# Attention feeding an MLP: weight loads placed between the first pairs' casts, transposes moved inside a pair, and the first MLP tile begun earlier

## The chip, the cores and the metric

The kernel runs on one core of a Trainium2 chip. The metric is the device time of one execution, in microseconds. Eight runs of the kernel before took 435.03 to 438.9 us, with a median of 437.28 us. The profile is of one execution that took 436.74 us; its recorded span is 435.0 us.

The core has five engines that work side by side, each through its own queue in order: PE (matrix products, with PEld for loading the stationary operand), DVE and ACT (elementwise work), POOL (elementwise work and DMA issues) and SP (DMA issues only). Sixteen DMA engines move the data.

## The reference

```python
scores = scale * np.matmul(q, k.transpose(0, 1, 3, 2))      # 8 batches, 12 heads, 448 x 448, head size 64
attn = np.exp(scores - max) / (sum + 1e-09)
attn_out = np.matmul(attn, v)                               # [8, 12, 448, 64]
x = attn_out.transpose(0, 2, 1, 3).reshape(3584, 768)
h = x @ w_in                                                # 768 x 2048
g = np.maximum(0.01 * h, h)
out = g @ w_out                                             # 2048 x 768
```

All inputs and the output are float32 in memory; the kernel multiplies in bf16. The kernel leaves out the subtraction of the maximum, whose factor cancels in the division, and gets the sum from a column of ones beside v.

## The kernel before, in words

**Units.** Two heads of one batch make a pair, so there are 48 pairs `u`, six to a batch. The MLP's 3584 rows are cut into eight tiles at multiples of 128: the first has 384 rows, the others 384 to 512. MLP tile i can begin when all six pairs of batch i have left their output, turned, in `xT`.

**A pair's way.** `load` brings q, k and v by three DMAs of 224 KB each on SP's queue (the very first k on ACT's). `cast` turns them to bf16 on POOL: q and k into `qkb` (L109, L110; 4 buffers), v into one of five v tiles (L111). q and k are then turned so that the head dimension lies on partitions: by PE in `transposes` (eight products into the single PSUM buffer `tr`, L159, then one DVE copy, L162) for the pairs below `NPE` = 10, by a DMA transpose on SP's queue for the rest. `scores` makes one 112-row chunk of scores for both heads (L171) in one of two PSUM buffers; `expo` takes its exponential on ACT (L180). There are four chunks, so four exponentials to a pair. `pv` multiplies them with v for one head (16 small products into the single buffer `pv`, L189), and DVE divides (L196, L197). `x_transposes` turns the pair's output into `xT`: by PE and `tr` again for pairs below 7 (L210, L211), by DMA from then on.

**Weights.** `w_in` and `w_out` are cast to bf16 by the DMA itself, issued from POOL's queue by `load_w` in eight pieces: four column quarters of `w_in`, then four row quarters of `w_out` (L123). One piece is issued ahead of the loop, one after each cast in slots 0, 1, 2, and the four `w_out` pieces in pairs 5 to 8.

**The order.** It is written out by hand. Each pair has eight slots, `s0` to `s7`, and slots of one `u` mix work of three pairs: scores of `u`, `pv` of `u-1`, x transposes of `u-2`, cast of `u+3`, load of `u+5`, and the PE transposes of `u+1` in the last slot. `steps` is the list of all slots. `begin[i]` is the step after which MLP tile i starts; from there its products (`mlp`, one product per `yield`) are dealt out evenly over the steps up to `begin[i+1]`. Tile 0 starts in pair 7 after its slot 1: `begin[0]` = 8 x 7 + 7 - 5 = 58. It is dealt out over 53 steps, first `h` for the 16 row blocks (L232, L237), then, for each 128 rows, two column halves of the output (L244, L249), and `store` on SP's queue.

**Buffers that set the order of transfers.** There are five load buffers of each of q, k and v, so SP can issue the load of pair u+5 when pair u is cast. The queue of SP is in order: a DMA transpose or a store in it stands ahead of the loads issued after it.

Of the kernel before, what the change touches and what calls it, by code (L numbers as in the profile page):

```python
# [9 lines left out]
F32 = mybir.dt.float32  # L10
BF16 = mybir.dt.bfloat16
# [5 lines left out]
def kernel(  # L17
# [9 lines left out]
    nc = tc.nc  # L27

    B, H, S, D = q.shape
    DM, DF = moe_w_in.shape  # L30
    P = 128
    HP = H // 2
# [3 lines left out]
    MD = DF // P  # L36
    NW = DM // 2
    NU = B * HP
    scale = 1.0 / float(D) ** 0.5

    cuts = [((b * S) // P) * P for b in range(B)] + [B * S]
# [3 lines left out]
    const_pool = ctx.enter_context(tc.tile_pool(name="const", bufs=1))  # L45
# [10 lines left out]
    o_pool = ctx.enter_context(tc.tile_pool(name="o", bufs=3))  # L56
# [4 lines left out]
    ps_mm = ctx.enter_context(tc.tile_pool(name="ps_mm", bufs=2, space=PSUM))  # L61
# [20 lines left out]
    w_out_sb = w_pool.tile([P, MD, DM], BF16)  # L82
    w_in_v = moe_w_in.rearrange("(ko ki) n -> ki ko n", ki=P)
    w_out_v = moe_w_out.rearrange("(ko ki) n -> ki ko n", ki=P)
# [6 lines left out]
    def load(u, queues=(nc.sync,) * 3):  # L91
        if u >= NU:
            return
        b, hp = divmod(u, HP)
        raw[u] = []
        for a, name, eng in zip((q, k, v), ("fq", "fk", "fv"), queues):
            t = ld_pool.tile([SC, 2, NSC, D], F32, name=name)
            eng.dma_start(  # L98
                out=t.rearrange("p h so d -> p h (so d)"),
                in_=a[b, 2 * hp:2 * hp + 2].rearrange("h (p so) d -> p h (so d)", so=NSC),  # L100
            )
            raw[u].append(t)

    def cast(u, by=(nc.gpsimd.tensor_copy,) * 3):
        if u >= NU:
            return
        fq, fk, fv = raw.pop(u)
        qk_sb[u] = cast_pool.tile([SC, 2, NSC, 2, D], BF16, name="qkb")
        by[0](qk_sb[u][:, 0].rearrange("p so h d -> p h so d"), fq)  # L109
        by[1](qk_sb[u][:, 1].rearrange("p so h d -> p h so d"), fk)  # L110
        by[2](v_sb[u % NV][:, :, :, :D], fv)  # L111

    w_steps = []
    for i in range(4):
        w_steps.append((w_in_sb[:, :, ts(i, DF // 4)], w_in_v[:, :, ts(i, DF // 4)]))
    for i in range(4):
        w_steps.append((w_out_sb[:, ts(i, MD // 4), :], w_out_v[:, ts(i, MD // 4), :]))

    def load_w(n=1):
        for _ in range(n):  # L120
            if w_steps:
                o, i = w_steps.pop(0)
                nc.gpsimd.dma_start(out=o, in_=i)  # L123

    load(0, (nc.sync, nc.scalar, nc.sync))
    for i in range(1, 5):
        load(i)
    ident = const_pool.tile([P, P], BF16)
    make_identity(nc, ident)
    for t in v_sb:  # L130
# [10 lines left out]

    x_t = {}

    NPE = 10

    def turn(dst, src):
        nc.sync.dma_start_transpose(out=dst.rearrange("p (c s) -> p c s", s=SC), in_=src)

    def dma_transposes(u):
        if NPE <= u < NU:  # L150
            turn(qkT[u % NQ][:, :QL], qk_sb[u].rearrange("p i so h d -> p (i so h d)"))

    def transposes(u):
        if u >= min(NPE, NU):
            return
        tr = ps_tr.tile([P, 2, S], BF16, name="tr")
        for i in range(2):
            for so in range(NSC):
                nc.tensor.transpose(  # L159
                    tr[:, i, ts(so, SC)], qk_sb[u][:, i, so], ident[:SC, :SC]  # L160
                )
        nc.vector.tensor_copy(qkT[u % NQ][:, :QL], tr.rearrange("p i s -> p (i s)"))  # L162
# [3 lines left out]
    def scores(u, c):  # L166
        ps = ps_s.tile([P, 2, 512], F32, name="sc")
        t = qkT[u % NQ]
        sc_t[u, c] = ps
        for j in range(2):  # L170
            nc.tensor.matmul(  # L171
                ps[:, j, :S],
                t[j * D:(j + 1) * D, S + c * SC:S + c * SC + P],
                t[j * D:(j + 1) * D, :S],
                start=True, stop=True,
            )

    def expo(u, c):
        e = e_sb[u % NE][:, :EL].rearrange("p (j c s) -> p j c s", j=2, c=NSC)
        nc.scalar.activation(e[:, :, c, :], sc_t.pop((u, c))[:SC, :, :S], AX.Exp, scale=scale)  # L180

    def pv(u, j):

        e, vt = e_sb[u % NE], v_sb[u % NV]
        ps = ps_pv.tile([P, NSC, D + 1], F32, name="pv")
        for qc in range(NSC):
            for c in range(NSC):
                at = (j * NSC + c) * S + qc * SC
                nc.tensor.matmul(  # L189
                    ps[:, qc, :], e[:, at:at + P], vt[:, j, c, :],  # L190
                    start=(c == 0), stop=(c == NSC - 1),
                )
        if j == 0:
            x_t[u] = x_pool.tile([SC, NSC, 2, D], BF16, name="x")
        rec = r_pool.tile([SC, NSC, 1], F32, name="rec")
        nc.vector.reciprocal(rec, ps[:SC, :, D:])  # L196
        nc.vector.tensor_mul(  # L197
            x_t[u][:, :, j, :], ps[:SC, :, :D], rec.to_broadcast([SC, NSC, D])
        )

    def x_transposes(u):
        b, hp = divmod(u, HP)
        at = b * S % NX
        dst = xT[:, hp, at:at + S]
        if u >= NPE - 3:
            turn(dst, x_t.pop(u).rearrange("p so h d -> p (so h d)"))
            return
        tr = ps_tr.tile([P, 2, S], BF16, name="tr")
        for so in range(NSC):
            nc.tensor.transpose(tr[:, 0, ts(so, SC)], x_t[u][:, so], ident[:SC, :SC])  # L210
        nc.vector.tensor_copy(dst, tr[:, 0, :])  # L211


    def store(o, t0):

        done = 0
        while done < P:
            b, j = divmod(t0 + done, S)
            so, p = divmod(j, SC)
            n = min(SC - p, P - done)  # L220
            dst = out[b * S:(b + 1) * S].rearrange("(p so) n -> so p n", so=NSC)
            nc.sync.dma_start(out=dst[so, p:p + n], in_=o[done:done + n, :])
            done += n

    def mlp(i):
        n = cuts[i + 1] - cuts[i]
        at = cuts[i] % NX
        h = h_pool.tile([P, MD, 4 * P], BF16, name="h")
        for m in range(MD):
            ps = ps_mm.tile([P, 4 * P], F32, name="mm")  # L230
            for kk in range(KD):
                nc.tensor.matmul(  # L232
                    ps[:, :n], w_in_sb[:, kk, ts(m, P)], xT[:, kk, at:at + n],
                    start=(kk == 0), stop=(kk == KD - 1),
                )
                if kk == KD - 1:
                    nc.scalar.activation(h[:, m, :n], ps[:, :n], AX.Prelu, alpha=0.01)  # L237
                yield n
        for c in range(n // P):
            o = o_pool.tile([P, DM], F32, name="o")  # L240
            for w in range(2):
                ps = ps_mm.tile([P, 4 * P], F32, name="mm")
                for m in range(MD):
                    nc.tensor.matmul(  # L244
                        ps[:, :NW], h[:, m, ts(c, P)], w_out_sb[:, m, ts(w, NW)],
                        start=(m == 0), stop=(m == MD - 1),
                    )
                    if m == MD - 1:
                        nc.vector.tensor_copy(o[:, ts(w, NW)], ps[:, :NW])  # L249
                    yield NW  # L250
            store(o, cuts[i] + c * P)


    def slots(u):

        on = u < NU

        def s0():
            if on:
                scores(u, 0)  # L260
                scores(u, 1)
                expo(u, 0)

        def s1():
            if on:
                expo(u, 1)
            if 2 <= u <= NU + 1:
                x_transposes(u - 2)
            dma_transposes(u + 2)

        def s2():
            if 1 <= u <= NU:
                pv(u - 1, 0)

        def s3():
            load(u + 5)

        def s4():
            if on:
                scores(u, 2)  # L280
                scores(u, 3)
                expo(u, 2)

        def s5():
            if on:
                expo(u, 3)
            cast(u + 3)
            if u <= 2 or 5 <= u <= 8:
                load_w()

        def s6():
            if 1 <= u <= NU:
                pv(u - 1, 1)

        def s7():
            if u + 1 < NU:
                transposes(u + 1)

        return [s0, s1, s2, s3, s4, s5, s6, s7]

    steps = [s for u in range(NU + 2) for s in slots(u)]

    begin = [8 * (HP * (i + 1) + 1) + 7 - 5 * (i == 0) for i in range(B)]
    assert begin[B - 1] == 8 * (NU + 1) + 7
    transposes(0)
    for s in steps[:begin[0]]:
        s()
    for i in range(B):
        work = steps[begin[i]:begin[i + 1]] if i + 1 < B else []
        n = cuts[i + 1] - cuts[i]  # L310
# [42 lines left out]
```

## Time and profile before

| | |
|---|---|
| median of 8 runs | 437.28 us |
| profiled execution | 436.74 us, span 435.0 us |
| PE busy | 410.2 us (94%), 3678 instructions |
| ACT busy | 230.0 us (53%) |
| DVE busy | 97.8 us (22%) |
| POOL busy | 91.3 us (21%) |
| read from memory, written to it | 45.61 MB, 11.01 MB |

A row by stage gives, after the stretch and its length, the busy time of each engine with its number of instructions, the granted clock of PE, the mean busy share of the DMA engines and the rate. A row of the time line gives the start, the length, the engine, the line of the program, the operation, its result and operand with sizes, the count, and in brackets the idle time of the engine before it and what ended it. Two successive products overlap in the record, so prices of PE work are best taken from start to start.

### The profile page before, as it was taken

How to read it: one execution, taken by the hardware profiler on the slowest of the kernel's cores; microseconds unless marked ns; L12 is line 12 of the kernel's file. 1: busy time of each engine (PE TensorE's matmuls, PEld its weight loads, DVE VectorE, ACT ScalarE, POOL GpSimd, SP SyncE). 2: the span in 40 equal slices, each digit the busy share in tenths (PEclk: the TensorE clock that was granted, in tenths of full speed). 3: DMA queues.
4: the chain of work that ended last, by engine and by line, in shares of the span. 5: the costliest groups of instructions: out<-in, count | busy, mean ns of one | idle time of the engine just before them, and what ended most of it. 6: DMA issues, size and time to landing. Idle time of an engine off the chain costs nothing.

```text
span 435.0 us, 8908 instructions
## 1 busy us (share of the span) xinstructions
PE 410.2 (94%) x3678; PEld 225.4 (52%) x3692; DVE 97.8 (22%) x266; ACT 230.0 (53%) x322; POOL 91.3 (21%) x168
## 2 busy tenths in 40 slices
PE   3767969999999999999999999999999999999995
PEld 1445535554455555554455555554445555554563
DVE  1343311321122211331123211331112311320021
ACT  4677645456743577447653377447654377304300
POOL 5535504231112113131112213122111200000000
PEclk9999997999999999999999999999999999999998
DMA  9999999876646775776656766786556440230022
GB/s 226 252 245 270 244 183 250 231 189 152 122 103 171 162 174 128 155 210 151 121 132 169 136 167 155 145 213 147 121 145 174 72 101 13 57 83 4 0 74 72
DMA packets 99273, 64.35 MB, mean 148 GB/s; under 512 B 58272, under 2 KB 95648, under 8 KB 99232
## 3 DMA queue, kind: packets, MB, share of 16 engines
q1 hardware_dynamic: 93744, 57.25, 55.8%
q0 software_dynamic: 5248, 6.29, 8.5%
q8 instruction: 29, 0.48, 0.5%
q10 hardware_dynamic: 240, 0.23, 0.2%
q14 instruction: 12, 0.10, 0.1%
HBM read 45.61 MB, written 11.01 MB: 130 GB/s over the span
## 4 chain that ended last, share of the span: by engine, by line
PE 84%; DMA 14%; issue 0%; POOL 0%; DVE 0%; SPq 0%; POOLq 0%
PE mm L244 34%; PE mm L232 32%; PE pv L189 9%; PE sc L171 9%; DMA fk<-in_k_dram 5%; DMA qkT<-qkb 4%; DMA fq<-in_q_dram 3%; DMA fv<-in_v_dram 2%; POOL qkb L110 0%; DVE o L249 0%; SPq L98 0%; POOLq L109 0%; POOL v L111 0%
## 5 line engine op out<-in xcount | busy, mean ns | idle before, releaser
L180 ACT ACTIVATE e<-sc 112x896 bf16<-112x896 f32 x192 | 167.8, 915 | 116.8 <-PE sc L171 116.6
L232 PE MATMUL mm<-xT,w_in_sb 128*128 128x384 bf16 (+1 forms) x754 | 161.8, 356 | 0.8
L244 PE MATMUL mm<-w_out_sb,h 128*128 128x384 bf16 x896 | 160.2, 326 | 0.0
L244 PEld LDWEIGHTS <-h 128*128 128x128 bf16 x896 | 81.6, 98 | 62.4 <-issue 14.1
L232 PEld LDWEIGHTS <-w_in_sb 128*128 128x128 bf16 x768 | 69.2, 98 | 72.1 <-issue 18.1
L237 ACT ACTIVATE h<-mm 128x384 bf16<-128x384 f32 (+1 forms) x128 | 69.8, 545 | 59.9 <-PE mm L232 59.7
L111 POOL CAST v<-fv 112x512 bf16<-112x512 f32 x48 | 29.6, 616 | 221.0 <-PE pv L189 210.3
L189 PEld LDWEIGHTS <-e 112*128 112x128 bf16 x1536 | 62.1, 99 | 15.0 <-issue 2.1
L171 PE MATMUL sc<-qkT 64*128 64x448 bf16 x384 | 56.1, 365 | 14.5 <-DVE qkT L162 7.0
L196 DVE RECIPROCAL rec<-pv 112x4 f32<-112x4 f32 x96 | 17.5, 182 | 222.4 <-PE pv L189 221.6
L189 PE MATMUL pv<-v,e 112*128 112x65 bf16 x1536 | 66.1, 195 | 0.0
L249 DVE COPY o<-mm 128x384 f32<-128x384 f32 x56 | 31.2, 557 | 89.4 <-PE mm L244 89.2
L197 DVE TENSOR_TENSOR x<-pv,rec 112x256 bf16<-112x256 f32 x96 | 40.7, 424 | 3.6 <-DVE rec L196 0.3
L171 PEld LDWEIGHTS <-qkT 64*128 64x128 bf16 x384 | 12.2, 95 | 46.9 <-issue 30.0
L109 POOL CAST qkb<-fq 112x512 bf16<-112x512 f32 x47 | 28.9, 614 | 26.2 <-DMA qkT<-qkb 14.7
L110 POOL CAST qkb<-fk 112x512 bf16<-112x512 f32 x47 | 28.8, 614 | 8.4 <-DMA fk<-in_k_dram 7.8
L159 PE MATMUL tr<-ident,qkb 112*128 112x112 bf16 x80 | 6.8, 238 | 4.8 <-DVE qkb L109 4.8
L159 PEld LDWEIGHTS <-qkb 112*128 112x128 bf16 x80 | 5.2, 110 | 5.6 <-DVE qkb L109 4.8
L162 DVE COPY qkT<-tr 128x896 bf16<-128x896 bf16 x10 | 6.2, 618 | 6.0 <-PE tr L159 5.9
L211 DVE COPY xT<-tr 128x448 bf16<-128x448 bf16 x7 | 2.7, 391 | 7.3 <-PE tr L210 7.3
L123 POOL DMA_DIRECT2D w_in_sb<-in_moe_w_in_dram x4 | 3.4, 852 | 0.0
L123 POOL DMA_DIRECT2D w_out_sb<-in_moe_w_out_dram x4 | 3.0, 743 | 0.0
(14 smaller groups left out, 8.1 us busy)
## 6 DMA issues: line engine op xcount, KB each, us to landing
fq<-in_q_dram SPq DMA_DIRECT2D x48, 224.0 KB, 3.7
fv<-in_v_dram SPq DMA_DIRECT2D x48, 224.0 KB, 4.0
fk<-in_k_dram SPq DMA_DIRECT2D x47, 224.0 KB, 3.9
w_in_sb<-in_moe_w_in_dram POOLq DMA_DIRECT2D x4, 768.0 KB, 12.9
w_out_sb<-in_moe_w_out_dram POOLq DMA_DIRECT2D x4, 768.0 KB, 16.0
out_dram<-o SPq DMA_DIRECT2D x8, 336.0 KB, 3.0
out_dram<-o SPq DMA_DIRECT2D x8, 288.0 KB, 2.8
out_dram<-o SPq DMA_DIRECT2D x8, 240.0 KB, 2.7
```

Of the source, the lines that this page charges most:

```text
L109: by[0](qk_sb[u][:, 0].rearrange("p so h d -> p h so d"), fq)
L110: by[1](qk_sb[u][:, 1].rearrange("p so h d -> p h so d"), fk)
L111: by[2](v_sb[u % NV][:, :, :, :D], fv)
L171: nc.tensor.matmul(ps[:, j, :S], t[j * D:(j + 1) * D, S + c * SC:S + c * SC + P], t[j * D:(j + 1) * D, :S], start=True, stop=True,)
L180: nc.scalar.activation(e[:, :, c, :], sc_t.pop((u, c))[:SC, :, :S], AX.Exp, scale=scale)
L189: nc.tensor.matmul(ps[:, qc, :], e[:, at:at + P], vt[:, j, c, :], start=(c == 0), stop=(c == NSC - 1),)
L196: nc.vector.reciprocal(rec, ps[:SC, :, D:])
L197: nc.vector.tensor_mul(x_t[u][:, :, j, :], ps[:SC, :, :D], rec.to_broadcast([SC, NSC, D]))
L232: nc.tensor.matmul(ps[:, :n], w_in_sb[:, kk, ts(m, P)], xT[:, kk, at:at + n], start=(kk == 0), stop=(kk == KD - 1),)
L237: nc.scalar.activation(h[:, m, :n], ps[:, :n], AX.Prelu, alpha=0.01)
L244: nc.tensor.matmul(ps[:, :NW], h[:, m, ts(c, P)], w_out_sb[:, m, ts(w, NW)], start=(m == 0), stop=(m == MD - 1),)
L249: nc.vector.tensor_copy(o[:, ts(w, NW)], ps[:, :NW])
```

## The change

There are six edits.

1. `w_out` is cut in four blocks of 8 row groups by half the columns, instead of four quarters of rows. A DMA of such a piece has rows of 384 values, not 768.
2. `load_w` moves from slot 5 to slot 3, ahead of the transposes there. One piece is still issued before the loop; then one in pair 2, two in pair 3, two in pair 4, two in pair 5.
3. The PE transposes of pair `u+1` move from the last slot to slot 3, between the two groups of scores of pair `u`. `NPE` goes from 10 to 12, so q and k of pairs 10 and 11, and the outputs of pairs 7 and 8, are turned by PE.
4. Fifteen products of a zeroed tile with itself are added on PE: nine before anything else, two after the first transposes, four after the first two score chunks. Their result is not used.
5. Pair 6, the first of batch 1, has slots of its own (`turning_slots`): both halves of `pv` of pair 5, the x transposes of pairs 4 and 5 and the transposes of pair 6 come first, and the scores of pair 6 after them. `begin[0]` becomes 8 x 6 + 3 = 51, so MLP tile 0 starts after the first scores of pair 6 and is dealt out over 60 steps.
6. For tile 0, the output halves are made in the order of their columns: the left half of all three 128-row blocks first, then the right half, with each block's store after its right half.

```diff
-        w_steps.append((w_out_sb[:, ts(i, MD // 4), :], w_out_v[:, ts(i, MD // 4), :]))
+        at = (slice(None), ts(i % 2, MD // 2), ts(i // 2, NW))
+        w_steps.append((w_out_sb[at], w_out_v[at]))
...
+    warm = const_pool.tile([P, 512], BF16)
+    nc.vector.memset(warm, 0.0)
+    def warm_up(n):
+        for _ in range(n):
+            ps = ps_mm.tile([P, 512], F32, name="mm")
+            nc.tensor.matmul(ps, warm[:, :P], warm, start=True, stop=True)
+    warm_up(9)
...
-    NPE = 10
+    NPE = 12
...
+        todo = [(c, w) for c in range(n // P) for w in range(2)]
+        if i == 0:
+            todo.sort(key=lambda cw: cw[1])
...
+    def turning_slots(u):
+        def s0():
+            pv(u - 1, 0)
+            x_transposes(u - 2)
+        def s1():
+            pv(u - 1, 1)
+            transposes(u)
+        def s2():
+            x_transposes(u - 1)
+        def s3():
+            scores(u, 0)
+            scores(u, 1)
+            expo(u, 0)
+            load(u + 5)
+        def s4():
+            expo(u, 1)
+            transposes(u + 1)
+        def s5():
+            scores(u, 2)
+            scores(u, 3)
+            expo(u, 2)
+            cast(u + 3)
+        def s6():
+            expo(u, 3)
+        return [s0, s1, s2, s3, s4, s5, s6, lambda: None]
...
+            if u == 0:
+                warm_up(4)
...
-            if 2 <= u <= NU + 1:
+            if 2 <= u <= NU + 1 and u - 2 not in (HP - 2, HP - 1):
                 x_transposes(u - 2)
...
             load(u + 5)
+            load_w({2: 1, 3: 2, 4: 2, 5: 2}.get(u, 0))
+            if u + 1 < NU and u + 1 != HP:
+                transposes(u + 1)
...
-            if u <= 2 or 5 <= u <= 8:
-                load_w()
...
-            if u + 1 < NU:
-                transposes(u + 1)
+            pass
...
-    begin = [8 * (HP * (i + 1) + 1) + 7 - 5 * (i == 0) for i in range(B)]
+    begin = [8 * (HP * (i + 1) + 1) + 7 for i in range(B)]
+    begin[0] = 8 * HP + 3
     transposes(0)
+    warm_up(2)
```

More of the change, by code (lines that the diff above doesn't have):

```diff
@@ L238, in mlp @@
                 yield n
[L239 to L251, printed above, removed]
+        todo = [(c, w) for c in range(n // P) for w in range(2)]
+        if i == 0:
+            todo.sort(key=lambda cw: cw[1])
+        o = {}
+        for c, w in todo:
+            if c not in o:
+                o[c] = o_pool.tile([P, DM], F32, name="o")
+            ps = ps_mm.tile([P, 4 * P], F32, name="mm")
+            for m in range(MD):
+                nc.tensor.matmul(
+                    ps[:, :NW], h[:, m, ts(c, P)], w_out_sb[:, m, ts(w, NW)],
+                    start=(m == 0), stop=(m == MD - 1),
+                )
+                if m == MD - 1:
+                    nc.vector.tensor_copy(o[c][:, ts(w, NW)], ps[:, :NW])
+                    if w == 1:
+                        store(o.pop(c), cuts[i] + c * P)
+                yield NW
+    def turning_slots(u):
[23 more added lines that the diff above has]
+        return [s0, s1, s2, s3, s4, s5, s6, lambda: None]
     def slots(u):
@@ L295, in s7 @@
         def s7():
-            if u + 1 < NU:
-                transposes(u + 1)
+            pass
         return [s0, s1, s2, s3, s4, s5, s6, s7]
-    steps = [s for u in range(NU + 2) for s in slots(u)]
-    begin = [8 * (HP * (i + 1) + 1) + 7 - 5 * (i == 0) for i in range(B)]
+    steps = [s for u in range(NU + 2) for s in (turning_slots if u == HP else slots)(u)]
+    begin = [8 * (HP * (i + 1) + 1) + 7 for i in range(B)]
+    begin[0] = 8 * HP + 3
     assert begin[B - 1] == 8 * (NU + 1) + 7
     transposes(0)
+    warm_up(2)
     for s in steps[:begin[0]]:
```

## The prediction

> **What bounds the kernel now.** I read the engine rows first, then PE's busy time by stage, then the chain of waits, then the time line where PE stops, then the DMA queues there. PE is busy for 410.2 of 435.0 us, so what can be won is its 24.8 idle us and whatever it ran at half clock. By stage (span, then busy time of PE, PEld, DVE, ACT, POOL, then granted clock, DMA share, GB/s):
>
> ```profile
> 0.00:40.00 40.00, 25.32 (x355) 15.75 (x356) 14.43 (x39) 26.06 (x31) 18.84 (x46) 1.00 1.10 246
> 40.00:60.30 20.30, 19.84 (x207) 11.47 (x203) 5.42 (x16) 15.13 (x25) 8.90 (x15) 1.00 1.15 225
> 60.30:64.40 4.10, 0.04 (x1) 0.00 (x0) 0.00 (x0) 0.24 (x1) 0.00 (x0) 0.90 1.16 209
> 64.40:70.80 6.40, 6.36 (x37) 3.13 (x39) 0.61 (x2) 2.70 (x4) 3.57 (x6) 0.53 1.19 261
> 70.80:430.20 359.40, 358.63 (x3088) 195.03 (x3101) 76.82 (x209) 185.86 (x263) 60.03 (x102) 1.00 0.56 131
> ```
>
> From 70.8 us PE never stops: nothing but PE work counts there. The losses are 14.7 us before 40, 4.1 at 60, half clock until 70.8, and a 4.8 us tail. DMA is full up to here.
>
> The losses before 40 us come once per pair; two pairs on PE and ACT:
>
> ```profile
> 23.96 0.56 PE L159 MATMUL tr<-ident,qkb 112*128 112x112 bf16 x8
> 25.39 0.55 PE L171 MATMUL sc<-qkT 64*128 64x448 bf16 x4 [0.87 <-DVE qkT L162]
> ...
> 21.36 3.34 ACT L180 ACTIVATE e<-sc 112x896 bf16<-112x896 f32 x4 [1.16 <-PE sc L171]
> 25.85 3.34 ACT L180 ACTIVATE e<-sc 112x896 bf16<-112x896 f32 x4 [1.15 <-PE sc L171]
> ```
>
> The transposes stand last in a pair, so the next pair's scores wait for their copy, and ACT idles 1.15 of every 4.49 us. The stop at 60 us is the DMA queue's, by the chain in order of time and the time line:
>
> ```profile
> 28.32 12.83 DMA fq<-in_q_dram
> ...
> 41.21 4.21 DMA fv<-in_v_dram
> 45.42 18.97 DMA qkT<-qkb
> ...
> 64.44 0.93 PE sc L171 x4
> ```
>
> ```profile
> 64.44 0.93 PE L171 MATMUL sc<-qkT 64*128 64x448 bf16 x4 [4.10 <-DMA qkT<-qkb]
> ```
>
> The first DMA transpose (pair 10, counted from 0) is issued at 45.42 and lands 19 us later, behind 13 pairs' loads and beside w_out. The packets of the hardware queue q1 (loads, transposes) and of q0 (weights), in the windows 8 to 12, 20 to 24, 48 to 52 and 56 to 64 us:
>
> ```profile
> q1 hardware_dynamic: 1081, 1.03, 110.4%
> q0 software_dynamic: 17, 0.02, 2.6%
> ...
> q0 software_dynamic: 486, 0.50, 73.1%
> q1 hardware_dynamic: 484, 0.46, 43.3%
> ...
> q0 software_dynamic: 392, 0.58, 79.1%
> q1 hardware_dynamic: 392, 0.37, 34.1%
> ...
> q0 software_dynamic: 822, 1.21, 93.1%
> q1 hardware_dynamic: 830, 0.24, 22.9%
> ```
>
> **What the Trainium skill says.** "DMA: Bandwidth & Descriptors", section "Queues, rings and completion order", has each engine go round its queues packet by packet; the trace agrees (486 to 484, 392 to 392). Section "Latency and other measured facts" puts a GpSimd transfer's first byte at about 1 us; here w_out is issued at 40.98 and q0 has only 229 packets in 44 to 48 us, which at 98 per us starts it near 45.6: I use 4.5 us. "TensorE: Matmul & The Clock Gate", Part 1 on the clock gate, says that an idle window of about 3.4 us halves the clock and as much steady work restores it; the trace agrees (0.53 after 4.1 idle us, full again after 6.4).
>
> **Prices.** DMA, from these lines: a 1 KB load packet 4.0/1081 = 3.7 ns; a load beside w_in 4.0/485 = 8.25 ns the two, so w_in 4.55; beside w_out 10.2, so w_out (1.5 KB) 6.5; a 256 B transpose packet 9.7 - 6.5 = 3.2. A pair's load is 672 packets, a w_in piece 768, a pair's qk transpose 896. w_out had 4 x 512 packets and gets 4 x 1024 of 0.75 KB: 3.25 ns each if bytes set the price, 6.5 if packets do; I take 3.5 (the line through 4.55 and 6.5). Check on the kernel before, to the end of w_out near 67.6: start 2.2, 13 loads 32.3, w_in 14.0, w_out 13.3, transposes of q/k (10) and x (7) 4.3, some 450 packets of the next load 1.7: 67.8.
> PE, start to start at full clock: two score chunks 0.48, one pv half 0.52, eight qk transposes 0.39, four x transposes 0.20, a 384-column product 0.164.
>
> **The change, part by part.**
>
> *Transposes between the score groups.* In pair u, PE now does scores 0 and 1, x, pv, the next pair's transposes, scores 2 and 3, pv. After exp 3 of the last pair ends at E, PE needs 0.1 + 0.24 (score 1), 0.2 (x), 0.52 (pv), about 0.1 (one tr bank: x's copy) and 0.39 before score 2, whose exp can start at E+2.0; ACT has done exps 0 and 1 at E+1.67. So a pair costs 3.34 + 0.35 = 3.7 us, not 4.49. Bounds: 3.34 (ACT alone) and 4.49. First exp at 7.2; pair 0 waits for pair 1's cast (8.2) before its third score and ends near 10.9. Pairs 1 to 4 at 3.74 end at 25.9, pair 5, which holds no transposes, at 29.2. The before has this point at 33.7. The casts allow it: before, q/k of pairs 3, 4, 5 are cast by 13.1, 17.9, 23.3, wanted at 15.8, 19.5, 23.3; w_in pieces 1 to 3 now come after the casts of pairs 4 and 5, so between 18.3 (end of w_in 0) and 24.2 loads run alone and pair 5 is cast by 21.8.
>
> *Warm-up.* The memset and fifteen products are new. Nine 512-column products at half clock (0.317 x 512/384 = 0.42) are 3.8 us from about 1.2, in front of transposes that started at 4.76: at most 0.3 late. Two more hide under the qkT copy (0.72 wait), four under the first exps; if still at half clock these four cost 1.7, of which 0.8 shows. Against that, pairs 0 to 2 ran at half clock (eight transposes 0.93 against 0.56). I take zero, -0.8 to +1.
>
> *Turning pair (u = 6).* Between E = 29.2 and MLP tile 0, one pv bank and one tr bank make a chain: pv half 0.5, reciprocal and multiply 0.18 + 0.42 with hand-overs 0.9, second half 0.5, its reciprocal and multiply to E+2.75, copy of pair 6's qkT 0.62 ahead of the x transposes, these 0.2, copy 0.39: MLP begins at E+4.2 = 33.4 instead of 40.05.
>
> *Sum.* From its MLP start the before needs 435.0 - 40.05 = 394.95. Taken off: the 4.10 stop, the half clock (scores 0.86 - 0.48, 15 products 4.59 - 2.46, pv 0.89 - 0.52: 2.9), two waits of 0.23 on the copies. Added: at 40.05 the before had done a pair of scores, transposes and a pv half more (0.96 + 0.39 + 0.52 = 1.9), and pairs 10, 11 and x of 7, 8 now turn on PE (2 x 0.39 + 2 x 0.20 = 1.2). So the end is 33.4 + 390.6 = 424.0, plus new stops. DVE's two longer copies (0.62) and two of 0.39 hide under PE work.
>
> *DMA.* w_in 1 is issued at 19.7 behind the fourth pair's v cast, and starts at 24.2; SP's queue still owes 4928 load packets up to pair 14, all ahead of the first transpose (pair 12). 2304 pairs with w_in at 8.25: 43.2. 2624 with w_out at 7.2: 62.1. 896 transposes at 6.7: 68.1, landing 69 to 71. The last 576 of w_out: 72.3, landed 73. When does PE want them? MLP 0 (192 products, 31.5 us) is spread over 60 steps. Pair 12 starts after 46: 24.2 + 13.0 of attention = 70.6. The fourth w_out piece is wanted at 47.5 steps, 72.0; the others 2 us or more after they land (w_in 43.2 against 52). So stops of about 1.5 us together; bounds 0 and 4.5 from the landing lags.
> The seven weight issues on POOL (0.74 to 0.96 each) go ahead of casts: two in a row delay pairs 6 to 8 by 1.6, which land later anyway. Behind them on POOL wait the v casts, and behind these SP's loads five pairs on.
> Taken from SP's queue are four transposes; of the three issued at 45.42, 55.57 and 61.85 each held SP for 4.1 to 6.2 us, and no load could be issued behind it. Pair 12's will do the same, but loads up to pair 14 are out by then.
> Stores of MLP 0 now come bunched; they cost nothing while SP runs ahead of PE, else up to 1 us.
>
> End: 425.5 us of span; 1.74 around it (436.74 against 435.0) gives 427.2, against 436.74. That run is 0.54 below the median of 437.28, so I say **427.5**.
>
> **Rivals.**
> 1. *The stop only moves* (15 in 100): more waits on weights and on pair 12, 4 to 8 us, and a half clock of up to 3. For it: DMA is full to 73 us and the front starts earlier; up to seven weight pieces stand on POOL's queue, where the trace shows at most four, and an issue that had to wait would hold casts. Against: two fewer transposes beside w_out. 431 to 436.
> 2. *The pair stays at 4.49* (10 in 100), because PE in order puts score 2 behind pv and transposes: MLP begins 4.5 later, and the stops vanish: about 430 to 431.
> 3. *Slower* (5 in 100): a 0.75 KB packet of w_out costs what a 1.5 KB one did, 6.5 ns. Then w_out ends at 43.2 + 14.7 + 4096 x 0.0065 = 84.5, 13 us late, with a half clock behind: 442. It decides from 5.7 ns. Against: w_in's 1 KB packets cost 4.55, nearly by bytes.
> 4. *No stop and a quick front* (8 in 100): 422 to 424.5.
>
> **How the numbers follow.** The forecast has 62 in 100 (424.5 to 430). Changes within 0.3% can't be told from none here. Faster 0.92 (forecast, rivals 1, 2, 4), within 0.3% 0.03 (the top of rival 1), slower 0.05. Range 423.5 to 433: it leaves out half of 4, half of 1 and all of 3.
>
> **What would show it.** Right: ACT's four exps every 3.7 us up to 26 us; PE's first w_in product at 33 to 34; no stop of 4 us and no clock of 0.5 near 60 to 80; the pair 12 transpose landing near 70; w_out's last packets at 72 to 73; PE ending near 421. Wrong: w_out's packets fewer than 125 per us beside loads, POOL sitting on a weight issue, or PE idle over 4 us after its MLP start.

## The result and the profile after

The changed kernel takes 427.62 us (median of 11 runs) against 437.27 us for the kernel before (32 runs). The ratio of the two over all their runs is 0.979, with a 95% interval of 0.977 to 0.982 (the medians alone divide to 0.978). The runs of the changed kernel lie between 426.05 and 432.12 us. The profiled execution took 427.74 us, its span is 425.9.

PE's stages after the change (stretch, length, busy time of PE, PEld, DVE, ACT, POOL, then granted clock, DMA share, GB/s):

```profile
0.00:34.10 34.10, 26.25 (x340) 15.27 (x341) 14.13 (x39) 22.25 (x27) 22.27 (x51) 0.98 1.08 246
34.10:36.20 2.10, 2.10 (x15) 1.41 (x14) 0.00 (x0) 1.50 (x2) 0.79 (x2) 0.52 1.18 245
36.20:72.80 36.60, 36.60 (x391) 21.23 (x389) 11.34 (x30) 25.77 (x38) 11.03 (x19) 1.00 1.22 240
72.80:421.10 348.30, 347.33 (x2978) 188.62 (x2992) 74.04 (x202) 180.32 (x256) 57.74 (x98) 1.00 0.55 131
421.10:425.90 4.80, 0.00 (x0) 0.00 (x0) 0.44 (x1) 0.00 (x0) 0.00 (x0) 0.93 0.29 82
```

The MLP begins at 34.09, and from 36.2 to the start of pair 12 at 72.80 PE is busy for 36.60 of 36.60 us. The 4.1 us stop and its half clock are gone; a shorter half clock of 3.4 us now lies across the MLP's start (0.52 in the second row). The tail is 4.8 us as before.

A pair on PE and ACT, from the time line:

```profile
19.38 0.55 PE L170 MATMUL tr<-ident,qkb 112*128 112x112 bf16 x8
19.87 0.55 PE L182 MATMUL sc<-qkT 64*128 64x448 bf16 x4
...
16.46 3.34 ACT L191 ACTIVATE e<-sc 112x896 bf16<-112x896 f32 x4 [0.48 <-PE sc L182]
20.34 3.34 ACT L191 ACTIVATE e<-sc 112x896 bf16<-112x896 f32 x4 [0.54 <-PE sc L182]
```

The transposes are those of the next pair, and the scores behind them belong to the pair that is under way, so they follow at once and wait for no copy. ACT's wait is 0.5 us a pair, not 1.15: 3.88 us from pair to pair. The DMA queues from 60 to 64 us (packets, MB, share of the DMA engines' time):

```profile
q0 software_dynamic: 582, 0.45, 71.0%
q1 hardware_dynamic: 583, 0.51, 49.1%
```

Two packets now take 4.0/582 = 6.9 ns against 10.2. With 3.7 for the load packet, w_out's 0.75 KB packet costs 3.2 ns, half of the 6.5 ns of the 1.5 KB one: bytes set its price here.

### The profile page after: what moved, and what is told of

It reads as the page before. It is cut to its first block, busy times and chain, and to the rows that moved or that the text cites. A ratio compares the mean times of both kernels' runs of the same rounds, so it can differ in the third digit from the quotient of the medians.

```text
span 425.9 us, 8982 instructions
## 1 busy us (share of the span) xinstructions
PE 412.3 (97%) x3716; PEld 226.5 (53%) x3731; DVE 99.9 (23%) x271; ACT 229.8 (54%) x322; POOL 91.8 (22%) x168
## 4 chain that ended last, share of the span: by engine, by line
PE 93%; ACT 2%; DMA 1%; issue 1%; DVE 1%; POOL 1%; SPq 0%; ACTq 0%
PE mm L243 35%; PE mm L260 35%; PE pv L200 11%; PE sc L182 10%; ACT e L191 2%; PE tr L170 1%; DMA fv<-in_v_dram 1%; PE tr L221 0%; DVE x L208 0%; POOL w_in_sb L124 0%; POOL qkb L109 0%; POOL v L111 0%; DVE rec L207 0%; POOL qkb L110 0%; DVE o L265 0%
## 5 line engine op out<-in xcount | busy, mean ns | idle before, releaser
L111 POOL CAST v<-fv 112x512 bf16<-112x512 f32 x48 | 29.6, 616 | 203.0 <-PE pv L200 158.0
L200 PEld LDWEIGHTS <-e 112*128 112x128 bf16 x1536 | 61.0, 98 | 16.1 <-DVE x L208 2.2
L200 PE MATMUL pv<-v,e 112*128 112x65 bf16 x1536 | 64.9, 194 | 1.4 <-DVE x L208 1.4
L182 PE MATMUL sc<-qkT 64*128 64x448 bf16 x384 | 54.6, 357 | 4.3 <-ACT e L191 3.2
L173 DVE COPY qkT<-tr 128x896 bf16<-128x896 bf16 x12 | 7.4, 620 | 7.2 <-PE tr L170 7.2
L170 PEld LDWEIGHTS <-qkb 112*128 112x128 bf16 x96 | 6.2, 103 | 2.4 <-DVE qkb L109 0.5
L136 PE MATMUL mm<-warm 128*128 128x512 bf16 x15 | 5.7, 531 | 1.2 <-DVE warm L131 1.2
L221 PE MATMUL tr<-ident,x 112*128 112x112 bf16 x36 | 3.5, 222 | 0.9 <-DVE qkT L173 0.9
## 6 DMA issues: line engine op xcount, KB each, us to landing
w_in_sb<-in_moe_w_in_dram POOLq DMA_DIRECT2D x4, 768.0 KB, 14.9
```

Source lines behind the costliest of these rows:

```text
L170: nc.tensor.transpose(tr[:, i, ts(so, SC)], qk_sb[u][:, i, so], ident[:SC, :SC])
L182: nc.tensor.matmul(ps[:, j, :S], t[j * D:(j + 1) * D, S + c * SC:S + c * SC + P], t[j * D:(j + 1) * D, :S], start=True, stop=True,)
L200: nc.tensor.matmul(ps[:, qc, :], e[:, at:at + P], vt[:, j, c, :], start=(c == 0), stop=(c == NSC - 1),)
```

## The experiments

Each time is a median, and each ratio is to runs of the kernel before on the same chip; its medians there were 436.2 to 437.3 us. "After" means the changed kernel. A difference from after is one of medians of runs on different chips, so the ratios with their intervals say whether it is clear of the spread. The idle products' results are not used, so no kernel here leaves out part of the computation.

### Parts undone, one at a time

**The turning pair undone.** Pair 6 gets ordinary slots.

```diff
-            if 2 <= u <= NU + 1 and u - 2 not in (HP - 2, HP - 1):
+            if 2 <= u <= NU + 1:
...
-            if u + 1 < NU and u + 1 != HP:
+            if u + 1 < NU:
...
-    steps = [s for u in range(NU + 2) for s in (turning_slots if u == HP else slots)(u)]
+    steps = [s for u in range(NU + 2) for s in slots(u)]
...
-    begin[0] = 8 * HP + 3
+    begin[0] = 8 * (HP + 1) + 2
```

> The turning pair is undone: pair 6 has the ordinary slots again, the scores of pair 6 come before both pv halves of pair 5, and MLP tile 0 begins after slot 1 of pair 7 (step 58); all else as after. Theory A (after the MLP start PE never stops, so only the work left at the start counts): the turning pair took 4.9 us from the last exponential of pair 5 (29.3) to the first product (34.1), with 1.9 us less PE work done than the ordinary order would have at about 34.3, and a half clock of 3.4 us. So without it 1.9 + about 1 us are saved: 424.5 to 426, against 427.6 for after. Theory B (the turning pair brings the MLP forward by a pair, which is where its part of the gain comes from): the MLP begins one pair (3.8 us) later and the kernel is 2 to 4 us slower: 430 to 432.

Measured: 428.02 us, ratio 0.980 (0.977 to 0.983), no different from after. Both theories miss. The waits of PE in its time line, where it had none in after:

```profile
71.48 0.55 PE L182 MATMUL sc<-qkT 64*128 64x448 bf16 x4 [1.17 <-DMA qkT<-qkb]
...
75.41 0.32 PE L260 MATMUL mm<-w_out_sb,h 128*128 128x384 bf16 x1 [0.49 <-DMA w_out_sb<-in_moe_w_out_dram]
```

Here the MLP began at 35.57 us, with 1.9 us more PE work behind it, at full clock. Against after, which began at 34.09 and lost about 1.0 us to the half clock, that is worth 1.9 + 1.0 - 1.5 = 1.4 us. The two waits, 1.7 us together, took it back: pair 12's transpose had landed 2.9 us early in after (69.9 against 72.8) and is now 1.2 late. This execution also had a half clock from 12.0 to 15.4 us that after's had not. In the run with two more pairs on PE below, which has the same front without that half clock, the MLP began at 34.65. The turning pair itself brought nothing that can be measured.

**The transposes back in the last slot.**

```diff
-            if u + 1 < NU and u + 1 != HP:
-                transposes(u + 1)
...
         def s7():
-            pass
+            if u + 1 < NU and u + 1 != HP:
+                transposes(u + 1)
```

> The transposes of the next pair go back to the last slot; all else as after. Theory A: ACT idles again about 1.15 us a pair, pair 5 ends near 32.8 instead of 29.3, MLP begins 3.5 later, no stop elsewhere: 430.5 to 431.5. Theory B (the front of after is set by the DMA queue, as in the kernel before): the transposed pair 12 lands at 70 anyway, no change: 427 to 428.

Measured: 433.79 us, ratio 0.991 (0.988 to 0.995), 6.2 us slower than after. Theory B falls; A names the direction and is at least 2.3 us short. In the profiled run pair 5's exponentials end at 32.92, as A has it, but the MLP starts at 38.42 (4.3 later than in after), because most of the turning pair now runs at half clock, which lasts 6.8 us and not 3.4:

```profile
34.30:41.10 6.80, 5.82 (x47) 3.71 (x47) 2.57 (x7) 1.72 (x2) 1.90 (x4) 0.50 1.18 248
```

Past the MLP's start the half clock lasts 2.7 us against 2.0 in after, which costs 0.3, and three waits of 0.23 for the copies of later pairs come back: 4.3 + 0.3 + 0.7 = 5.3, where the spans differ by 5.7 (431.6 against 425.9).

**No warm-up products.**

```diff
-    warm_up(9)
...
-            if u == 0:
-                warm_up(4)
...
-    warm_up(2)
```

> All fifteen warm-up products and their zeroed tile are left out; all else as after. Theory A (prediction): about nothing, since the clock comes up by itself in the front and the waits there are ACT's: 427 to 428.5. Theory B (PE at half clock makes the pairs of the front PE-bound, so that pairs 0 and 1 lose 1.5 us each until the clock is up near 16 us): 429.5 to 431.

Measured: 430.62 us, ratio 0.983 (0.980 to 0.987). The medians are 3.0 us apart, in the range of theory B. The size isn't settled: the interval overlaps that of after (to 0.982), two of the six executions took 427.8 and 427.9 us, and the means differ by 1.7 us only. The traces show the mechanism. ACT's exponentials of the front without the products, and the stage at the MLP's start:

```profile
9.59 3.34 ACT L188 ACTIVATE e<-sc 112x896 bf16<-112x896 f32 x4 [0.53 <-PE sc L179]
14.19 3.58 ACT L188 ACTIVATE e<-sc 112x896 bf16<-112x896 f32 x4 [1.26 <-PE sc L179]
18.38 3.34 ACT L188 ACTIVATE e<-sc 112x896 bf16<-112x896 f32 x4 [0.61 <-PE sc L179]
```

```profile
33.90:40.80 6.90, 6.11 (x30) 2.72 (x31) 1.76 (x4) 3.24 (x5) 2.52 (x5) 0.51 1.18 245
```

In after, the same three groups start at 9.16, 12.64 and 16.46. By the clock's record PE comes to full clock at 16.9 us instead of 5.4. Until then PE's way from one pair to the next (scores 0.50 from start to start, pv 0.86, transposes 0.87) no longer fits under ACT; the first two pairs lose 1.1 and 0.4 us, not 1.5 each. The MLP starts 1.93 later (36.02). Past that start the half clock lasts 4.8 us, not 2.0, which costs another 1.4: 3.3 together, where the spans differ by 3.2 (429.1 against 425.9).

**w_out in row quarters,** with the old order of tile 0's outputs and the new times of issue.

```diff
-        at = (slice(None), ts(i % 2, MD // 2), ts(i // 2, NW))
-        w_steps.append((w_out_sb[at], w_out_v[at]))
+        w_steps.append((w_out_sb[:, ts(i, MD // 4), :], w_out_v[:, ts(i, MD // 4), :]))
...
-        if i == 0:
-            todo.sort(key=lambda cw: cw[1])
```

> w_out goes in row quarters again and the outputs of tile 0 are made in the old order; the times of issue are those of after. Theory A: the first output product needs all four pieces within 2.5 us of 60.7, and the last lands at 72, so PE stops some 9 us there and runs at half clock for up to 6 after it: 436 to 440. Theory B (the pieces' shape is off the path): 427 to 428.

Measured: 434.52 us, ratio 0.991 (0.987 to 0.995), 6.9 us slower than after. B falls, and A's size was too large. The shape of the pieces and the order of the outputs were undone together, so which of the two would matter alone was not tried. PE's wait for w_out, and the products after it at half clock:

```profile
65.69 1.12 PE L257 MATMUL mm<-w_out_sb,h 128*128 128x384 bf16 x4 [2.50 <-DMA w_out_sb<-in_moe_w_out_dram]
...
67.50 2.27 PE L257 MATMUL mm<-w_out_sb,h 128*128 128x384 bf16 x7
```

I had the last quarter land at 72, near where the last column piece lands in after (72.8), and it landed at 65.7. The two queues move equal numbers of packets, so the one with larger packets moves more bytes, and the loads pay: from 52 to 56 us 398 packets of w_out and 396 of the loads carry 0.59 and 0.37 MB, in after 579 and 579 carry 0.44 and 0.55 MB. The stop is 2.5 us, with 3.4 us of half clock behind it. The profiled execution, at 430.94, is the quickest of this kernel's seven. One other takes as long, five take 2.0 to 4.4 us more, and where those lose it was not seen.

**NPE back to 10.**

```diff
-    NPE = 12
+    NPE = 10
```

> NPE back to 10; all else as after. PE has 1.2 us less work. Theory A: pair 10's transpose stands behind 13 loads and lands near 60.5 against 59.5 wanted, pair 11's near 73 against 66.5 wanted: stops of 5 to 7 us and a half clock behind them: 432 to 436. Theory B (the DMA transposes are hidden): 426 to 427.

Measured: 435.44 us, ratio 0.997 (0.995 to 0.999), 7.8 us slower than after. Theory A holds:

```profile
65.24 1.30 PE L260 MATMUL mm<-w_out_sb,h 128*128 128x384 bf16 x7
71.73 0.93 PE L182 MATMUL sc<-qkT 64*128 64x448 bf16 x4 [5.19 <-DMA qkT<-qkb]
```

It is pair 11 that waits; pair 10's transpose came in time. A half clock of 3.4 us follows it.

### Parts alone, in the kernel before

**The transposes between the score groups, and nothing else.**

```diff
             load(u + 5)
+            if u + 1 < NU:
+                transposes(u + 1)
...
         def s7():
-            if u + 1 < NU:
-                transposes(u + 1)
+            pass
```

> The kernel before with one edit alone: the next pair's transposes stand between the two score groups. Theory A (the transposed pair 10 is set by what the DMA queue has to move before it): pairs go at 3.8 us instead of 4.5, the MLP begins some 4 to 5 us earlier, and the stop before pair 10 grows by as much, since its transpose lands near 64 all the same: 436 to 438, no gain. Theory B (the pair's order alone makes the front shorter): 4 to 5 us faster, 432 to 433.

Measured: 436.56 us against 437.0, ratio 0.999 (0.997 to 1.001): no gain. Theory A's result holds, but not its way. The pairs do go at 3.8 to 3.9 us from 14 to 26 us, yet the MLP starts at 39.24, only 0.8 earlier than before and not 4 to 5. The front loses its gain at pair 7, whose transposes wait for POOL's cast of k, and this cast waits for its load:

```profile
35.09 0.37 PE L159 MATMUL tr<-ident,qkb 112*128 112x112 bf16 x4 [1.47 <-POOL qkb L110]
...
65.65 0.93 PE L171 MATMUL sc<-qkT 64*128 64x448 bf16 x4 [5.95 <-DMA qkT<-qkb]
```

```profile
34.00:40.00 6.00, 4.89 (x55) 2.97 (x56) 2.15 (x6) 3.45 (x4) 1.85 (x3) 0.72 1.16 261
40.00:59.70 19.70, 19.10 (x197) 10.94 (x194) 4.76 (x14) 14.14 (x23) 9.34 (x15) 1.00 1.15 233
59.70:65.60 5.90, 0.00 (x1) 0.00 (x0) 0.00 (x0) 0.21 (x1) 0.00 (x0) 0.76 1.16 207
```

That cast starts at 34.41 us here and at 34.11 in the kernel before, so it was the DMA that set it. A half clock from 35.5 to 38.9 follows (0.72 in the first row). What is left of the gain goes into the stop before pair 10, which ends at 65.65 where it ended at 64.44: whatever PE saves ahead of it, the DMA queue sets when pair 10 may go on. In after the same cast starts at 28.98, without a wait for its load. Three pieces of w_in are issued only after the casts of pairs 4 and 5 there, so from 20 to 24 us no packet of weights moves beside the loads:

```profile
28.98 0.63 POOL L110 CAST qkb<-fk 112x512 bf16<-112x512 f32 x1
...
q1 hardware_dynamic: 1129, 1.08, 112.6%
```

In the kernel before, 484 packets of loads moved in these 4 us, beside 486 of w_in. That the new times of issue are what makes the order's gain possible is read from these traces; no run undoes them alone. The same order that is worth 6.2 us inside after is worth nothing here.

**NPE 12, and nothing else.**

```diff
-    NPE = 10
+    NPE = 12
```

> The kernel before with one edit alone: NPE is 12, so pairs 10, 11 and x of 7, 8 are turned by PE. Theory A (the DMA transposes beside the weights are what cost the before its stop and half clock): the stop of 4.1 and the half clock of 2.9 go, 1.2 of PE work comes, and up to 2 us of stop on the last row quarter of w_out, which lands near 67: 431 to 433. Theory B (the DMA queue as a whole sets the front, whoever turns the pairs): no change, 436 to 438.

Measured: 433.11 us, ratio 0.992 (0.989 to 0.995), 3.7 us faster, just above the upper edge of A; B falls. The trace kept of this kernel is of an execution of 2315.19 us, in which a product of the MLP took over four times as long as in the others, so nothing is read from it: that the stop and the half clock went is argued from the time alone.

### Looking for a faster one

**Idle products in the turning pair,** to hold the clock.

```diff
             x_transposes(u - 2)
+            warm_up(4)
...
             transposes(u)
+            warm_up(4)
```

> Eight more idle products (512 columns, four after each of the first two groups of the turning pair) fill PE's waits there; all else as after. Theory A: the half clock from 32.7 to 36.1 us goes, the products hide in waits of 0.5 to 0.9 us: about 1.2 us less, 426 to 427. Theory B (the clock window is not filled by this, or the fillers push the chain): no change or up to 1 us more.

Measured: 426.94 us, ratio 0.978 (0.974 to 0.981). The half clock at the MLP's start is gone in the profiled run, and in those of the two runs below that have the same products, so the mechanism is as A has it, but 0.7 us against after lies inside both intervals and isn't a settled gain. This profiled run, one of the longest of its eight, had a half clock from 11.5 to 14.9 us instead, and a wait of 1.20 us for an x transpose ahead of MLP tile 1.

**That wait removed, too:** the outputs of pairs 9 to 11 turned by PE.

```diff
-        if u >= NPE - 3:
+        if u >= NPE:
```

> The turning pair with eight idle products, and the outputs of pairs 9, 10 and 11 also turned by PE; q and k of pairs 12 on stay with the DMA. Theory A (MLP tile 1 waits 1.2 us for the DMA transpose of pair 11's output, which stands behind stores and loads on SP's queue): that wait goes for 0.6 us of PE work: 426 to 426.5. Theory B (the wait is of the one profiled execution only): 427 to 428.

Measured: 427.78 us, ratio 0.980 (0.978 to 0.983). B's number holds. The wait for x is gone, and a wait of 0.6 us for w_out's last piece stands in the profiled run instead. Whether the wait for x was only of that one execution is not shown, since the kernel with the eight idle products has a trace of that one only.

**Two more pairs on PE, without the turning pair.**

```diff
-    NPE = 12
+    NPE = 14
...
-        if u >= NPE - 3:
+        if u >= NPE - 2:
...
```

(The other lines are those of the turning pair undone, above.)

> Without the turning pair, and pairs 12, 13 and x of 9 to 11 turned by PE too. Theory A (what the turning pair's absence saves was taken back by the wait for transposed pair 12 and by w_out's last piece, 1.7 us in the run without it): the wait for pair 12 of 1.2 goes, 1.4 us of PE work comes, w_out's wait stays: 427.5 to 428.5. Theory B (further DMA waits behind pair 12 were hidden in it): 425.5 to 427.

Measured: 428.09 us, ratio 0.981 (0.977 to 0.984). Theory A: PE no longer waits for pair 12, but for w_out's last piece it does, and its extra work eats the rest:

```profile
75.26 0.32 PE L260 MATMUL mm<-w_out_sb,h 128*128 128x384 bf16 x1 [1.31 <-DMA w_out_sb<-in_moe_w_out_dram]
```

**The same edit, with the turning pair and its idle products.**

> The turning pair with eight idle products, and pairs 12, 13 and x of 9 to 11 turned by PE too. Theory A (with the clock held, only a wait of 1.2 us for x's transpose before MLP tile 1 is left): that wait goes and 1.4 us of PE work comes: 426.5 to 427.5, no gain over the idle products alone (426.9). Theory B (waits for DMA transposes cost more in most executions than in the profiled one): 425 to 426.

Measured: 428.09 us, ratio 0.980 (0.977 to 0.984). Neither number holds; it is nearer A. The profiled run has no DMA wait after the MLP's start, and nothing was won for PE's 1.4 us.

**A second bank for the turning pair's pv,** x ahead of pair 6's q and k, four idle products, NPE 14.

```diff
...
             x_transposes(u - 2)
+            pv(u - 1, 1, ps_mm.tile([P, 512], F32, name="mm")[:, :NSC * (D + 1)])
+            warm_up(4)
 
         def s1():
-            pv(u - 1, 1)
+            x_transposes(u - 1)
+
+        def s2():
             transposes(u)
-
-        def s2():
-            x_transposes(u - 1)
...
-    begin[0] = 8 * HP + 3
+    begin[0] = 8 * HP + 2
```

> As the last, but in the turning pair the second pv half goes to a bank of the MLP's, so that it doesn't wait for the first half's division; the x transposes come before the copy of pair 6's q and k; MLP tile 0 begins before pair 6's transposes; four idle products. Theory A (the turning pair is a chain of waits for one pv bank and one tr bank): the first MLP product starts about 3 us after pair 5's last exponential instead of 4.8, 1.5 to 2 us are saved: 425 to 426. Theory B (DMA takes it back: w_out's last piece lands at 73 and is wanted at 72): 426.5 to 427.5.

Measured: 429.92 us, ratio 0.984 (0.980 to 0.988), 2.3 us more than after by the medians, against both theories; the two intervals overlap a little. From the first pv half (32.38) to the first MLP product (36.34) it took 3.96 us against 4.68 in after, and pair 6's scores were still to do (0.48). Together with 1.4 us for two more pairs on PE, the edit had nothing to win. The profiled run, the longest of the six, also came late to the turning pair, with a half clock from 22.7 to 29.6 us in the front; whether the others did is open.

So none of the variants is clearly faster than after.

## Why the prediction was right

The forecast of 427.5 us held, with 427.62 measured. The mechanism held: end = MLP start + the PE work left + stops. That the total came so close is luck in part: the MLP's start and the half clock across it were 1.7 us short in the forecast, and the 1.5 us of stops didn't come.

- **Pair order.** 3.7 us a pair was forecast. Pair 1 took 3.48 and the three pairs after it 3.82 to 3.88, in part because eight transposes took 0.49 us from start to start ahead of the scores, not 0.39. The quick pair 1 made up for that, so pair 5's exponentials ended at 29.28, where 29.2 was said. Alone, in the kernel before, the same edit gives nothing, since the loads come too late for it; the forecast had the loads come early enough in the changed kernel, and they did.
- **Warm-up.** "I take zero" is the step that failed. Leaving the products out costs 3.0 us by the medians and 3.2 by the profiled spans. The total came out right because the forecast's 3.7 us a pair from the second pair on took full-clock durations: the warm-up's gain stood in the sum under the pair order's name. A cost didn't show: the first exponential starts at 6.97 us with the products and at 7.34 without them. The bound on the gain, 0.8 us, was too small, since the MLP's start alone comes 1.9 earlier.
- **Turning pair.** E+4.2 was forecast and E+4.8 measured (29.28 to 34.09). The chain's waits dropped the clock at 32.7 us, and its last two links before the MLP, the x transposes and the first scores, took 0.47 and 0.86 us from start to start instead of 0.20 and 0.48. That half clock was not in the sum; it costs about 1 us more past the start (half of the 2.1 us in the second stage row). The starting point, 33.4, was 0.7 low, nearly all for the same reason.
- **Stops.** 1.5 us forecast, none measured. Pair 12's transpose landed at 69.9, in the 69 to 71 forecast, and w_out's last packet came at 72.3, as said. PE came later than forecast (pair 12 at 72.8, not 70.6; w_out's last piece near 75, not 72.0), so it found both there.
- **Sum.** 34.1 + 390.6 + 1.0 = 425.7 against a span of 425.9; the forecast was 33.4 + 390.6 + 1.5 = 425.5. Its last step doesn't add up: 427.2 and 0.54 are 427.8, and 427.5 takes only half of the 0.54.
- **Rivals.** 3 falls by the packet price of 3.2 ns. 2 falls by 3.88 us a pair. 1, that the stop only moves, is what happens when one of the two edits that make room is missing: 5.2 us of stop with NPE 10, 2.5 with row quarters. The edit on NPE was priced for its PE work and its packets, but I did not say that it decides between nearly the whole gain and almost none.

By the medians, the parts undone cost 6.2, 3.0, 6.9, 7.8 and 0.4 us, 24 together against a gain of 9.7. They depend on each other: PE's front and DMA's front both end near 70 us, so each edit on one side is worth something only while the other side keeps up. The new times of issue of the weights were not undone in any run.

## What to carry to other kernels

Where two queues both reach a common point late, an edit to one is to be priced against the other's arrival there, which can make the same edit worth 6 us or nothing. Cut a late transfer so that its pieces come in the order of use. In a latency-bound front, count what half clock does to every link before calling a warm-up free.

## What was not expected of the hardware

The half clock doesn't need a stop of PE. The clock's record changes in steps of 3.4 us, and in the two cases below a 3.4 us stretch in which PE was busy for only 1.9 to 2.0 us is followed by one at half clock, although no single wait in it was over 0.9 us. Three stretches of after in a row, then four of the run with the transposes in the last slot:

```profile
25.90:29.30 3.40, 2.46 (x42) 1.62 (x41) 1.60 (x5) 3.37 (x5) 3.40 (x6) 1.00 1.18 241
29.30:32.70 3.40, 1.94 (x44) 1.75 (x45) 2.03 (x6) 0.00 (x0) 3.40 (x6) 1.00 1.18 246
32.70:36.10 3.40, 3.34 (x21) 1.75 (x21) 0.40 (x2) 1.72 (x2) 1.30 (x3) 0.50 1.18 245
```

```profile
20.70:24.10 3.40, 2.01 (x34) 1.31 (x32) 1.78 (x6) 2.56 (x4) 2.31 (x5) 0.99 1.13 283
24.10:27.50 3.40, 3.40 (x39) 2.01 (x36) 1.00 (x3) 2.44 (x3) 3.40 (x6) 0.51 1.18 241
27.50:30.90 3.40, 2.46 (x45) 1.64 (x42) 1.88 (x6) 2.33 (x4) 3.10 (x5) 1.00 1.18 245
30.90:34.30 3.40, 1.86 (x39) 1.39 (x37) 1.26 (x5) 2.02 (x3) 2.16 (x4) 0.99 1.18 244
```

1.94, 2.01 and 1.86 are followed by 0.50 or 0.51; 2.46 is not. The busy time alone doesn't decide, though. The run with NPE 10 dropped the clock after a stretch with 2.05 us (27.4 to 30.8), and the run with row quarters kept it after one with 2.05 (28.5 to 31.9). With NPE 10 it was also kept after a stretch with only 1.7 (64.9 to 68.3), and dropped one stretch later, in which PE did nothing. PE's busy times are partly modelled, so no bound can be given from these records. The Trainium skill ("TensorE: Matmul & The Clock Gate", Part 1) speaks of an idle window of 3.4 us, and further down in the same part of a kernel whose clock went up and down because of short idle times alone. The length agrees, and here a window that was 59% busy was enough.

Where such a drop falls can differ between executions of the same work. Nine of the profiled kernels have the same front up to 11 us. By the clock's record PE came to full clock at 4.6 to 5.1 us in three of them, and these had a half clock from about 11.5 to 15 us; in the six others it came at 5.3 to 7.1 us, and these had none there.
